# Moving a product, its hash and its place in a step of a fused attention and mixture-of-experts kernel

## Chip, cores and metric

The kernel runs on one core of a Trainium2 chip. The metric is the device time of one execution in microseconds (us); three runs of the kernel before have a median of 731.03 us (730.82 to 731.37).

## Reference

Two batches of 8 heads, 768 positions and 64 dimensions go through attention restricted by a hash: `proj` gives 6 sign bits per query and key, and a pair counts only where all bits agree.

```python
q_bucket = np.sum((np.einsum('bhsd,dk->bhsk', q, proj) > 0) * powers, axis=-1)   # k alike
scores = np.where(mask, scale * q @ k.T, -1e9); attn = softmax(scores); attn @ v
```

The result, 1536 rows of 512, goes through 4 dense experts of 512 x 1024 x 512 with a ReLU, and the outputs are summed with row weights `p = domain_probs / sum`.

## The kernel before

**Tiling.** A head is worked on in 6 tiles of 128 queries; a tile is a *step*, and heads are counted 0 to 15 over both batches (8 to 15 are the second batch). `attention()` (line 589) is a generator: at step i it walks the letters of `ORDER` (line 45), each letter a stage with its own lag (lines 21 to 32) behind the scores, so several heads are in flight.

- S (`stage_s`, 397): scores of a tile on TensorE, 4 matmuls into a `big` PSUM buffer (2 of them); VectorE reads it with the mask's minimum (L409).
- E (420): exponential on ScalarE (L425) with the row sums.
- N (430): reciprocals of a head's row sums (L436, L437), written out as a `row` from the SP queue (L439). R (441): the rows read back, spread over 64 partitions (L450).
- Heads 0 to 8 are *mixed* (`LIGHT_FROM = 9`): T (457) turns a tile of probabilities on TensorE with 6 matmuls against the identity (L470), and ScalarE and VectorE copy it to a `pt` buffer.
- Heads 9 to 15, the *late* ones, turn by another way: X (481) transposes 32 x 32 blocks on VectorE (L490) and after three tiles writes them to a scratch tensor (`scr`, L496); Y (502) reads them back in four DMAs (L507) into a `pt` buffer. There are 3 `pt` buffers; a read-back waits until the product of the head before has freed its buffer.
- V (514): the product of probabilities and values, 24 matmuls in column tiles (L525) into `pv`. For mixed heads it comes in two parts at lags 4 and 6 after the head's last tile, for late heads at once at lag 8. U (534) copies `pv` out (L552, L554); M (556) multiplies with the reciprocals on GpSimd (L565).
- P: one step of `prep_head` (301) for the next head, on the turned inputs `xt`: the high part on ScalarE (L330) with three GpSimd copies, the low part on VectorE (L333), the *hash* (four small matmul passes in column tiles into `hps`, L346), its Sign on ScalarE (L356), and the mask rows on GpSimd (L361, L369). P also issues the loads of q, k (L206, twice removed head) and v (L222).

**Order of work.** Instructions are issued to each engine in the order in which the program is written (`manual_schedule`), so engines and the SP queue, which issues nearly every DMA, are in-order lists. Until the first batch's attention is done the main loop (line 1018) only steps attention; then the experts of batch 0 (`moe`, 774) run with the attention of batch 1 between them. Each `yield` gives a cost; after each block of 12 matmuls (1960 for the first layer, 2600 for the second) the loop at line 1034 steps attention while its summed yields are below the experts' times `n_att / n_moe` = 112404 / 250240. A step's scores yield 1363, a turning by T 654, a head's prep of a late head 978 in all, a step after the last tile 2500.

**Weights.** `split_w` (684) turns a loaded weight tile `ws` (512 KB, two buffers) into a high part (VectorE cast, L699) and a low part (GpSimd, L692); its calls stand between the blocks, and two of seven issue the next load on SP (`load_w`, L681). Load (u, i, c) is chunk c of layer i+1 for unit u.

Of the kernel before, what the change touches and what calls it, by code (L numbers as in the profile page):

```python
# [8 lines left out]
F32 = mybir.dt.float32  # L9
# [10 lines left out]
ATT_PACE = 1.0  # L20
LAG_E = 1
SPLIT_AT = (1, 0)
HASH_AT = (3, 1)
LAG_N = 3
LAG_R = ((6, 4), (7, 6))
LAG_T = 3
LAG_X = 2
LAG_Y = 4
LAG_V = ((4, 6), (8,))
LAST_V = (4, 5)  # L30
LAG_U = (3, 1)
LAG_M = (10, 10)
# [9 lines left out]
W_SPLIT = 40  # L42
W_STEP = 6
PREP_AT = 0
ORDER = "TXSUVMEYNRP"
LIGHT_FROM = 9
DRAIN = 2500
SPLIT_FIRST = 3
# [3 lines left out]
def tile_lsh_attention__then__domain_moe(  # L52
# [52 lines left out]
    def one(name):  # L105
        return ps1.tile([P, 512], F32, tag="one", name=name)
# [15 lines left out]
    def two(t):  # L122
        return t.rearrange("p (a n) -> p a n", a=2)
# [107 lines left out]
    def copy_pool(dst, src):  # L231
        nc.gpsimd.tensor_scalar(out=dst, in0=src, scalar1=1.0, scalar2=1.0, op0=ALU.mult, op1=ALU.mult)
# [63 lines left out]
    def turn_blocks(b, h):  # L296
        tqk = loaded.pop((0, b, h))
        xts[b, h] = ld.tile([P, S], F32, tag="tqk", name="xt")
        nc.vector.transpose(out=xts[b, h], in_=tqk.rearrange("p c r d -> p (c r d)"))

    def prep_head(b, h):
        second = (b, h) == (0, 1)
        q1, al, ah, k2 = stack_tiles(b, h)

        def copies():
            for rows in (slice(0, D), slice(D, P)):
                copy_pool(q1[rows], ah[0:D].bitcast(F32))
            copy_pool(k2[0:D], ah[D:P].bitcast(F32))

        if second:  # L310
            for ps, sl in zip(in_psum, halves):
                split_half(ah[:, sl], al[:, sl], ps[:, :NH])
            copies()
            yield 654
            yield 0
            ps = [one("hps1") for _ in range(2)]
            for j, (w, a) in enumerate(((phi, ah), (plo, ah), (phi, al))):
                for i, sl in enumerate(halves):
                    nc.tensor.matmul(ps[i][:MKE, :NH], w, a[:, sl], start=j == 0, stop=j == 2)
            copy_pool(ah[0:D], al[D:P].bitcast(F32))  # L320
            for i, sl in enumerate(halves):
                nc.scalar.activation(
                    k2[D:MKE, sl], ps[i][D:MKE, :NH], ACTF.Sign, bias=sgn_bias[D:MKE], scale=SGN_SCALE
                )
            yield 978
        else:
            xt = xts.pop((b, h))
            for _ in range(SPLIT_AT[not mixed(b, h)]):
                yield 0
            nc.scalar.activation(two(ah), two(xt), ACTF.Copy, scale=qk_scale)  # L330
            copies()
            yield 0
            nc.vector.scalar_tensor_tensor(  # L333
                out=two(al),
                in0=two(xt),
                scalar=qk_scale,
                in1=two(ah).bitcast(F32),
                op0=ALU.mult,
                op1=ALU.subtract,
            )  # L340
            copy_pool(ah[0:D], al[D:P].bitcast(F32))
            for _ in range(HASH_AT[not mixed(b, h)] - SPLIT_AT[not mixed(b, h)] - 1):
                yield 0
            hps = one("hps")
            for i, sl in enumerate(halves):
                nc.tensor.matmul(  # L346
                    hps[i * D : i * D + MKE - D, :NH],
                    pf[:, : MKE - D],
                    xt[:, sl],
                    start=True,  # L350
                    stop=True,
                    tile_position=(0, i * D),
                )
            for i, sl in enumerate(halves):
                rows = slice(i * D, i * D + MKE - D)
                nc.scalar.activation(  # L356
                    k2[D:MKE, sl], hps[rows, :NH], ACTF.Sign, bias=sgn_bias[rows], scale=SGN_SCALE
                )
            if not mixed(b, h):
                yield 978  # L360
        nc.gpsimd.tensor_scalar(  # L361
            out=al[D:MKE],
            in0=k2[D:MKE].bitcast(F32),
            scalar1=1.0,
            scalar2=bit_mul[D:MKE],
            op0=ALU.add,
            op1=ALU.mult,
        )
        copy_pool(k2[MQ:MQE], al[MK:MKE].bitcast(F32))  # L369
        yield 978 if mixed(b, h) and not second else 0  # L370

    xhi = {}
    xlo = {}
# [17 lines left out]
    def mixed(b, h):  # L391
        return b * H + h < LIGHT_FROM
# [121 lines left out]
    def stage_v(b, h, part, n_parts):  # L514
        if part == 0:
            pvs[b, h] = one("pv")
        ps = pvs[b, h]
        n = NT // n_parts
        for c in range(part * n, (part + 1) * n):
            for g in range(2):  # L520
                rows = slice(g * D, (g + 1) * D)
                dst = ps[rows, :GN]
                if not heavy(b, h, g * G):
                    dst = dst.rearrange("p (a q) -> p a q", q=32)
                nc.tensor.matmul(  # L525
                    dst,
                    vvs[b, h][:, c],
                    pts[b, h, g][c],
                    start=c == 0,
                    stop=c == NT - 1,  # L530
                    tile_position=(0, g * D),
                )
# [47 lines left out]
    def v_lags(b, h):  # L580
        return LAST_V if (b, h) == (0, H - 1) else LAG_V[not mixed(b, h)]

# [6 lines left out]
    def attention():  # L589
        n = len(seq)  # L590
        prep = [iter(())]

        def do(op, i):
            if op == "N":
                j = i - LAG_N
                if 0 <= j < n:
                    stage_n(*seq[j])
            elif op == "R":
                for b in range(B):
                    for odd in range(2):  # L600
                        j = i - LAG_R[b][odd]
                        if 0 <= j < n and (seq[j][0], seq[j][1] % 2) == (b, odd):
                            stage_r(*seq[j])
            elif op == "T":
                j = i - LAG_T
                if 0 <= j < n and heavy(*seq[j]):
                    stage_t(*seq[j])
                    return 654
            elif op == "X":
                j = i - LAG_X  # L610
                if 0 <= j < n and not heavy(*seq[j]):
                    stage_x(*seq[j])
            elif op == "Y":
                j = i - LAG_Y
                if 0 <= j < n and j % G == G - 1 and not heavy(*seq[j]):
                    b, h, t = seq[j]
                    stage_y(b, h, t // G)
            elif op == "S":
                if i < n:
                    b, h, t = seq[i]  # L620
                    if t == 0:
                        x = hseq.index((b, h))
                        prep[0] = prep_head(*hseq[x + 1]) if x + 1 < len(hseq) else iter(())
                    stage_s(b, h, t)
                    return 652 + 4270 // NT
                return DRAIN
            elif op == "V":
                for bh, lag in ended(i):
                    for part, at in enumerate(v_lags(*bh)):
                        if lag == at:  # L630
                            stage_v(*bh, part, len(v_lags(*bh)))
            elif op == "U":
                for bh, lag in ended(i):
                    if lag == u_lag(*bh):
                        stage_u(*bh)
            elif op == "M":
                for (b, h), lag in ended(i):
                    for g in range(NT // G):
                        if h % 2 and lag == (u_lag(b, h) if (b, h) == (0, H - 1) else LAG_M[b] + g):
                            stage_m(b, h, g)  # L640
            elif op == "E":
                j = i - LAG_E
                if 0 <= j < n:
                    stage_e(*seq[j])
            elif op == "P":
                if i < n:
                    b, h, t = seq[i]
                    c = next(prep[0], None) if t >= PREP_AT else None
                    x = hseq.index((b, h))
                    if t == NT - 1 and x + 2 < len(hseq) and in_blocks(*hseq[x + 2]):  # L650
                        turn_blocks(*hseq[x + 2])
                    if t == QK_AT and x + 2 < len(hseq):
                        load_qk(*hseq[x + 2])
                    if t == NT - 1 and x + 1 < len(hseq):
                        load_v(*hseq[x + 1])
                    return c
            return None

        for i in range(n + LAG_M[1] + 3):
            for op in ORDER:  # L660
                c = do(op, i)
                if c is not None:
                    yield c
# [410 lines left out]
```

## Time and profile before

| | |
|---|---|
| median of 3 runs | 731.03 us |
| profiled execution | 729.12 us, span of its instructions 727.4 us |
| mean granted TensorE clock | 0.997 |
| busy: TensorE, VectorE, ScalarE, GpSimd | 711.5, 483.0, 296.6, 303.0 us |
| chain that ended last, by engine | PE 88%, DVE 3%, DMA 3%, ACT 2% |
| DMA | 83.05 MB, 41% of 16 engines on the SP queue |

The first batch's attention takes the first 131 us; batch 0's experts with batch 1's attention reach to about 470 us, and the experts of batch 1 fill the rest. Busy times overlap; matmuls are pipelined with modelled ends, so a busy TensorE is not TensorE at its peak. PE is TensorE, PEld its weight loads, DVE VectorE, ACT ScalarE, POOL GpSimd, and SPq the DMA queue of SyncE. A line number such as L525 is a line of the kernel. In the chain each piece is followed back to what released it.

### The profile page before, as it was taken

The page shows a single profiled execution, that of the slowest core. Times are in us where ns is not written, and L with a number is a line of the kernel's source. Part 1 is how long each engine was busy: PE and PEld are TensorE (multiplying, and loading weights), DVE is VectorE, ACT ScalarE, POOL GpSimd, SP SyncE. Part 2 cuts the span into 40 slices and gives each one's busy share as a digit, 9 for nine tenths or more (in the row PEclk, how much of TensorE's full clock was granted, in tenths as well). Part 3 has the DMA queues.
Part 4 walks back from the last instruction along what each step waited for, and adds up shares of the span by engine and source line. Part 5 has one row for each costly group of instructions (what it writes and reads, how often), then busy time and mean ns, then how long its engine had stood idle before and what let it go on. Part 6 is the DMA issues. An engine that isn't in the chain of part 4 may idle for free.

```text
span 727.4 us, 10195 instructions
## 1 busy us (share of the span) xinstructions
PE 711.5 (98%) x3786; PEld 602.5 (83%) x3786; DVE 483.0 (66%) x800; ACT 296.6 (41%) x588; POOL 303.0 (42%) x283
## 2 busy tenths in 40 slices
PE   8999999999999999999979999999999999999998
PEld 6766766887978878798768889898998989899896
DVE  6898898456857566668524333986768576685863
ACT  6888888432433324323111111543425334352440
POOL 6359577413354253424213243933434243342420
PEclk9999999999999999999999999999999999999999
DMA  5323253227858869786466121142113221112202
GB/s 146 66 46 88 58 117 80 39 77 187 232 138 225 234 175 236 212 267 195 134 199 163 37 71 67 59 146 87 59 59 87 58 87 58 59 59 88 87 1 87
DMA packets 88641, 83.05 MB, mean 114 GB/s; under 512 B 53008, under 2 KB 55568, under 8 KB 88592
## 3 DMA queue, kind: packets, MB, share of 16 engines
q1 hardware_dynamic: 87568, 82.08, 41.0%
q8 instruction: 30, 0.49, 0.3%
q10 hardware_dynamic: 1024, 0.33, 0.2%
q14 instruction: 19, 0.16, 0.1%
HBM read 62.68 MB, written 19.71 MB: 113 GB/s over the span
## 4 chain that ended last, share of the span: by engine, by line
PE 88%; DVE 3%; DMA 3%; ACT 2%; POOL 1%; issue 1%; SPq 1%; DVEq 0%; POOLq 0%; ACTq 0%
PE mps L731 12%; PE mps L732 12%; PE mps L733 12%; PE pv L525 8%; PE mps L791 5%; PE mps L792 5%; PE mps L793 5%; PE ptps L470 4%; PE sps L404 4%; PE sps L402 4%; DMA ws<-in_moe_w_dram 3%; PE mps L946 2%; PE mps L942 2%; PE mps L945 2%; PE pd L942 2%; PE pa L946 2%
## 5 line engine op out<-in xcount | busy, mean ns | idle before, releaser
L731 PE MATMUL mps<-w2hi,hh 128*128 128x512 f32 (+1 forms) x388 | 151.0, 389 | 0.0
L733 PE MATMUL mps<-w2hi,hl 128*128 128x512 f32 (+1 forms) x388 | 150.5, 388 | 0.0
L732 PE MATMUL mps<-w2lo,hh 128*128 128x512 f32 (+1 forms) x388 | 150.4, 388 | 0.0
L725 DVE SCALAR_TENSOR_TENSOR acc<-mps,pe,acc 128x512 f32<-128x512 f32 (+1 forms) x85 | 63.0, 741 | 70.9 <-PE mps L733 70.4
L425 ACT ACTIVATE p<-p,nb 128x768 f32<-128x768 f32 x96 | 89.5, 933 | 35.6 <-DVE p L409 35.1
L797 ACT ACTIVATE hh<-mps 128x384 fp32r<-128x384 f32 x64 | 31.4, 491 | 169.8 <-PE mps L793 169.8
L409 DVE TENSOR_SCALAR_CACHE_REDUCE p<-sps 128x768 f32<-128x768 f32 x96 | 90.3, 942 | 15.1 <-PE sps L404 13.5
L791 PE MATMUL mps<-xs,w1hi 128*128 128x384 f32 x256 | 87.6, 342 | 4.7 <-DVE hl L798 4.7
L792 PE MATMUL mps<-xs,w1hi 128*128 128x384 f32 x256 | 86.6, 338 | 0.6 <-POOL xs L570 0.6
L793 PE MATMUL mps<-xs,w1lo 128*128 128x384 f32 x256 | 86.6, 338 | 0.0
L733 PEld LDWEIGHTS mps<-w2hi,hl 128*128 128x128 f32 x388 | 72.9, 188 | 15.7
L928 POOL TENSOR_TENSOR w2lo<-ws,w2hi 128x512 fp32r<-128x512 f32 x32 | 40.6, 1289 | 108.3 <-ACT w2hi L927 108.3
L731 PEld LDWEIGHTS mps<-w2hi,hh 128*128 128x128 f32 x388 | 72.9, 188 | 15.0 <-issue 1.2
L732 PEld LDWEIGHTS mps<-w2lo,hh 128*128 128x128 f32 x388 | 72.9, 188 | 13.9
L692 POOL TENSOR_TENSOR w1lo<-ws,w1hi 128x512 fp32r<-128x512 f32 x32 | 41.2, 1290 | 84.9 <-DVE w1hi L699 76.8
L692 POOL TENSOR_TENSOR w2lo<-ws,w2hi 128x512 fp32r<-128x512 f32 x32 | 41.2, 1288 | 82.5 <-DVE w2hi L699 66.3
L798 DVE SCALAR_TENSOR_TENSOR hl<-mps,hh 128x384 fp32r<-128x384 f32 x64 | 35.4, 555 | 59.1 <-ACT hh L797 58.8
L525 PE MATMUL pv<-pt,tv 128*64 128x384 f32 x288 | 67.3, 492 | 0.0
L402 PE MATMUL sps<-ah,q 128*128 128x384 f32 x192 | 54.0, 362 | 1.8 <-DVE p L409 1.8
L791 PEld LDWEIGHTS mps<-xs,w1hi 128*128 128x128 f32 x256 | 48.6, 190 | 8.2 <-DVE hl L798 5.0
L887 POOL TENSOR_TENSOR w1lo<-ws,w1hi 128x512 fp32r<-128x512 f32 x24 | 37.1, 1547 | 36.5 <-ACT w1hi L883 22.5
L470 PEld LDWEIGHTS ptps<-ident,p 128*128 128x128 f32 x324 | 36.4, 140 | 18.3 <-ACT p L425 8.2
(137 smaller groups left out, 1392.2 us busy)
## 6 DMA issues: line engine op xcount, KB each, us to landing
ws<-in_moe_w_dram SPq DMA_DIRECT2D x64, 512.0 KB, 4.0
scr<-t SPq DMA_DIRECT2D x14, 1152.0 KB, 8.6
pt<-scr SPq DMA_DIRECT2D x56, 288.0 KB, 6.1
tv<-in_v_dram SPq DMA_DIRECT2D x16, 192.0 KB, 3.7
tqk<-in_q_dram SPq DMA_DIRECT2D x30, 96.0 KB, 3.0
out_dram<-acc SPq DMA_DIRECT2D x11, 256.0 KB, 2.0
tqk<-in_k_dram SPq DMA_DIRECT2D x28, 96.0 KB, 3.1
rdb<-row SPq DMA_DIRECT2D x14, 192.0 KB, 6.2
```

Of the source, the lines that this page charges most:

```text
L402: nc.tensor.matmul(ps[:, i, :NH], q1[:, sl], k1[:, i * NH : (i + 1) * NH], start=True, stop=False)
L409: nc.vector.tensor_scalar(out=two(pt), in0=ps[:, :, :NH], scalar1=MASKED, scalar2=MASKED, op0=ALU.min, op1=ALU.min, accum_out=nb,)
L425: nc.scalar.activation(pt, pt, ACTF.Exp, bias=nb, scale=-1.0, accum_out=dens[b, h, r][:, o : o + 1])
L470: nc.tensor.transpose(ps[:, c * P : (c + 1) * P], pt[:, (a + c) * P : (a + c + 1) * P], ident)
L525: nc.tensor.matmul(dst, vvs[b, h][:, c], pts[b, h, g][c], start=c == 0, stop=c == NT - 1, tile_position=(0, g * D),)
L692: nc.gpsimd.tensor_tensor(out=lo[:, c - 1], in0=st[c - 1], in1=hi[:, c - 1].bitcast(F32), op=ALU.subtract)
L731: nc.tensor.matmul(ps, hh[:, ts], w2hi[:, f, cs], start=n == 0, stop=False)
L732: nc.tensor.matmul(ps, hh[:, ts], w2lo[:, f, cs], start=False, stop=False)
L733: nc.tensor.matmul(ps, hl[:, ts], w2hi[:, f, cs], start=False, stop=n == FC - 1)
L791: nc.tensor.matmul(ps[:, :SB], w1hi[:, kk, fs], xhi[b, kk][:, sl], start=kk == 0, stop=False)
L792: nc.tensor.matmul(ps[:, :SB], w1hi[:, kk, fs], xlo[b, kk][:, sl], start=False, stop=False)
L793: nc.tensor.matmul(ps[:, :SB], w1lo[:, kk, fs], xhi[b, kk][:, sl], start=False, stop=kk == KD - 1)
```

## The change

- `LAG_V` of late heads goes from 8 to 7 and V moves ahead of S in `ORDER`. `u_lag` follows the product, so U of late heads goes from 9 to 8; M, N, R, X, Y and the loads keep their lags.
- The hash of late heads moves from the second step of their prep to the first, beside the high part; the Sign follows it at once.
- For mixed heads the hash's matmuls are put on a list (`due`) at the end of the step in which the low part is made, and are issued in the next step's V, that is after T and the product and ahead of S; the Sign stays where it was.
- The yields of a prep change: late heads 654 + 978 in place of 978 in all, mixed heads 654 + 978 + 978 in place of 978. The number of yields is the same.

```diff
-HASH_AT = (3, 1)
+HASH_AT = (2, 0)
-LAG_V = ((4, 6), (8,))
+LAG_V = ((4, 6), (7,))
-ORDER = "TXSUVMEYNRP"
+ORDER = "TXVSUMEYNRP"
+    due = []
+    hashed = {}
+
+    def hash_of(b, h, xt):
+        hps = one("hps")
+        for i, sl in enumerate(halves):
+            nc.tensor.matmul(
+                hps[i * D : i * D + MKE - D, :NH],
...
+        hashed[b, h] = hps
+
+    def sign_of(b, h):
+        hps = hashed.pop((b, h))
+        for i, sl in enumerate(halves):
+            rows = slice(i * D, i * D + MKE - D)
+            nc.scalar.activation(
+                heads[b, h][3][D:MKE, sl], hps[rows, :NH], ACTF.Sign, bias=sgn_bias[rows], scale=SGN_SCALE
+            )
...
             xt = xts.pop((b, h))
...
+            late = b * H + h > H
+            steps = {}
+            steps.setdefault(SPLIT_AT[late], []).append("hi")
+            steps.setdefault(SPLIT_AT[late] + 1, []).append("lo")
+            steps.setdefault(HASH_AT[late], []).append("hash")
+            for at in range(max(steps) + 1):
+                if at:
+                    yield 654 if at == 1 else 0
+                for what in steps.get(at, ()):
...
+                    elif late:
+                        hash_of(b, h, xt)
+                        sign_of(b, h)
+                    else:
+                        due.append((b, h, xt))
+            yield 978
+            if not late:
+                sign_of(b, h)
...
-        yield 978 if mixed(b, h) and not second else 0
+        yield 0 if second or b * H + h > H else 978
...
                         if lag == at:
                             stage_v(*bh, part, len(v_lags(*bh)))
+                while due:
+                    hash_of(*due.pop())
```

## Rows read from the trace of the kernel before

**Rows 1.** Waits of TensorE in 130:430 (us in total, times, longest us)

```profile
PE mps L791 <- DVE hl L798: 4.7, 1, 4.7
PE sps L402 <- DVE p L409: 1.5, 2, 1.2
```

**Rows 2.** Windows (length, busy by engine (count), granted clock, DMA share, GB/s)

```profile
80.00:100.00 20.00, 18.98 (x124) 12.79 (x120) 18.17 (x34) 16.36 (x37) 17.85 (x19) 1.00 0.26 57
...
280.00:300.00 20.00, 18.51 (x102) 16.19 (x102) 18.60 (x33) 8.47 (x17) 10.35 (x9) 1.00 0.82 223
...
360.00:380.00 20.00, 15.33 (x83) 12.12 (x83) 3.66 (x6) 2.34 (x5) 1.46 (x2) 0.97 0.61 181
380.00:400.00 20.00, 20.00 (x96) 18.01 (x95) 9.54 (x18) 1.97 (x4) 7.55 (x6) 0.95 0.62 148
```

**Rows 3.** Chain that ended last, 355:385 (start us, us, what)

```profile
361.35 4.07 PE pv L525 x24
...
368.39 9.13 DMA ws<-in_moe_w_dram
...
377.62 0.14 DVE w2hi L699
...
378.56 0.66 PE mps L791
```

**Rows 4.** Timeline of the SP queue, 130:420 (start us, us)

```profile
164.69 0.38 SPq L681 DMA_DIRECT2D ws<-in_moe_w_dram  x1
165.18 1.83 SPq L507 DMA_DIRECT2D pt<-scr  x4
...
219.71 0.59 SPq L439 DMA_DIRECT2D row<-rd  x1
220.41 0.38 SPq L681 DMA_DIRECT2D ws<-in_moe_w_dram  x1
220.89 1.95 SPq L507 DMA_DIRECT2D pt<-scr  x4
...
237.59 1.75 SPq L507 DMA_DIRECT2D pt<-scr  x4
...
271.16 0.51 SPq L681 DMA_DIRECT2D ws<-in_moe_w_dram  x1
...
365.39 1.73 SPq L507 DMA_DIRECT2D pt<-scr  x4
```

**Rows 5.** Chain in 255:300, pieces of the repeating blocks

```profile
257.92 0.35 PE sps L402 x2
...
258.87 0.23 PE mps L732
...
291.31 0.17 PE mps L792
```

**Rows 6.** Chain in 200:215, a hash right behind a product

```profile
209.06 0.65 PE hps L346 x4
```

**Rows 7.** Timeline of VectorE round the reciprocal of head 10

```profile
216.13 0.75 DVE L725 SCALAR_TENSOR_TENSOR acc<-mps,pe,acc 128x512 f32<-128x512 f32 x1 [1.64 <-PE mps L733]
...
218.04 0.19 DVE L437 RECIPROCAL rd<-den 128x6 f32<-128x6 f32 x1
```

**Rows 8.** L507 to landing, of four reads: windows 163:168, 220:223, 236:240

```profile
DMA to landing us min/median/max: 4.4/5.7/7.1
...
DMA to landing us min/median/max: 6.2/7.3/8.5
...
DMA to landing us min/median/max: 3.4/5.0/6.3
```

**Rows 9.** Timeline of TensorE round a hash that stands alone (start us, us)

```profile
141.87 0.34 PE L793 MATMUL mps<-xs,w1lo 128*128 128x384 f32 x1
...
142.92 0.44 PE L791 MATMUL mps<-xs,w1hi 128*128 128x384 f32 x1
143.20 0.34 PE L792 MATMUL mps<-xs,w1hi 128*128 128x384 f32 x1
```

More of the change, by code (lines that the diff above doesn't have):

```diff
@@ L299, in turn_blocks @@
         nc.vector.transpose(out=xts[b, h], in_=tqk.rearrange("p c r d -> p (c r d)"))
+    due = []
[5 more added lines that the diff above has]
+                hps[i * D : i * D + MKE - D, :NH],
+                pf[:, : MKE - D],
+                xt[:, sl],
+                start=True,
+                stop=True,
+                tile_position=(0, i * D),
+            )
[6 more added lines that the diff above has]
+                heads[b, h][3][D:MKE, sl], hps[rows, :NH], ACTF.Sign, bias=sgn_bias[rows], scale=SGN_SCALE
+            )
     def prep_head(b, h):
@@ L327, in prep_head @@
             xt = xts.pop((b, h))
[L328 to L360, printed above, removed]
+            late = b * H + h > H
+            steps = {}
+            steps.setdefault(SPLIT_AT[late], []).append("hi")
+            steps.setdefault(SPLIT_AT[late] + 1, []).append("lo")
@@ new lines, in prep_head @@
+            steps.setdefault(HASH_AT[late], []).append("hash")
[3 more added lines that the diff above has]
+                for what in steps.get(at, ()):
+                    if what == "hi":
+                        nc.scalar.activation(two(ah), two(xt), ACTF.Copy, scale=qk_scale)
+                        copies()
+                    elif what == "lo":
+                        nc.vector.scalar_tensor_tensor(
+                            out=two(al),
+                            in0=two(xt),
+                            scalar=qk_scale,
+                            in1=two(ah).bitcast(F32),
+                            op0=ALU.mult,
+                            op1=ALU.subtract,
+                        )
+                        copy_pool(ah[0:D], al[D:P].bitcast(F32))
+                    elif late:
[3 more added lines that the diff above has]
+                        due.append((b, h, xt))
```

## The prediction, made before the kernel after was run

> **What bounds the kernel now.** I read the share of each engine first, then the windows, the waits of TensorE, the chain through its longest wait, and last the DMA issues of the SP queue. TensorE (PE) works almost without a break: between 130 and 430 us it waits for long only once, 4.7 us for `hl` [rows 1]. The windows place the idle time [rows 2]: 1.49 us in 280:300, 4.67 us in 360:380, and in the first batch 1.02 us in 80:100. So this change can gain only what such holes hold, and lose whatever new holes it opens.
>
> The chain shows how the 4.7 us came about [rows 3]. The product of head 14 (L525) runs 361.35 to 365.4; SP's L507, which reads probabilities back into a `pt` buffer that this product must free, follows at 365.39; behind it in SP's order stand a write to scratch and the weight load L681 at 368.39, which takes 9.13 us to land. VectorE, in order, sits in the cast L699 of those weights, `hl` behind it comes late, and PE resumes at 378.56. The hole of 280:300 is the same figure one cycle earlier: `ws` issued at 271.16 behind L507 [rows 4]. After the long hole the granted clock is 0.97 and 0.95 of full over two windows [rows 2], that is PE at 1.2 instead of 2.4 GHz for about 3.2 us, or 0.08 x 20 = 1.6 us lost.
>
> **How the order moves.** Positions below are us of PE work since the mixture experts began, worked out from the yields: an expert block of 12 matmuls is 12 x 0.17 or 12 x 0.23, a score tile twice 0.35 [rows 5], a product 4.07 [rows 3], a hash 0.65 [rows 6]; attention is stepped while its own counts are under 0.449 of the experts' (1,960 or 2,600 a block). So a late step with its scores, 1,363 counts, comes once per 3,035 expert counts, some 1.3 blocks or 3.3 us, and with its share of products, hashes and prep about every 5 us. The walk of the kernel before puts head 14's product at 226.3; plus 135 it is the 361.35 of the chain. Two things act on it. LAG_V 8 to 7, with V ahead of S, brings a product a step and a score tile forward. But a late head now yields 654 + 978 where it yielded 978, so a head costs 9,810 counts instead of 9,156 and the experts run 7% further per head. Together the products of heads 9 to 15 move from 73.3, 101.6, 132.5, 163.6, 194.6, 226.3, 265.5 to 66.4, 98.1, 131.1, 162.2, 195.3, 223.5, 263.4: little against the experts, and head 13's is even later. What changes is the order on SP.
>
> **The two weight waits (gain).** Before, the first read-back of head 12 and its scratch write stand ahead of weight load (3,1,0), and that read-back needs head 11's product, still a step away. After, the load comes at 131.1, ahead of the read-back at 138.6. Behind a scratch write issued near 127 it lands by 137, taking the 10.0 us of the load at 271.16 [rows 4]; its cast stands at 141.4. Head 15's read-back and load (5,1,0) swap alike: issue near 219.5, landing by 229.5, cast at 232.4. Both waits go, with 4.4 and 2.9 us to spare: -1.5 - 4.7 - 1.6 = -7.8 us.
>
> **The read-backs of the same head (loss).** A head's second read-back is ready only when its reciprocals are written (L439, ahead of it on SP), and now has one step less before its product. Before, the end of a block to the end of the reciprocal took about 2.1 us on VectorE (acc at 216.13, L437 until 218.23 [rows 7]); the row went out at 219.71 because SP was held by `tqk` loads, and the four reads at 220.89 [rows 4]. The last of four reads is issued about 1.3 us after the first. Landing, counted from the first issue, took 1.3 + 6.3 = 7.6 us (the four at 237.59), and with a weight load just ahead 1.3 + 7.1 = 8.4 (at 165.18) to 1.4 + 8.5 = 9.9 (at 220.89) [rows 4, 8]. By the walk, with 2 to 3 us for VectorE and 0.4 per issue, the four reads of heads 9 to 14 begin 7.0, 9.1, 7.7, 8.4, 10.2 and 9.3 us before PE reaches the product. Heads 9 and 12 have a weight load directly ahead of them: waits of 1.4 to 2.9 and 0 to 1.5. Head 10 has one further ahead (I take 0.2), head 13 has one but also the room, heads 11 and 14 have none. I take 2.0 + 0.2 + 0 + 0.8 + 0 + 0 = +3.0 us; the bounds are 0.6 (7.6 for all) and 8.0 (9.9 for all). Behind a waiting product on PE stand S and every later block; VectorE, ScalarE and the experts' evictions wait with it.
>
> A wait of 2 us before a product is between the 1.0 us holes that left the clock at 1.00 [rows 2] and the 4.7 us one that did not; I take no drop. The Trainium skill (TensorE: Matmul & The Clock Gate, Part 1) has it that the throttled state is the default and that activity releases it; a drop behind head 9's wait would by that cost about the 1.6 us again and make the forecast 729.2.
>
> **The late hash (loss).** Four hashes (heads 12 to 15) stood directly behind a product; now S and an expert block lie between. Behind a product a hash takes 0.65 [rows 6]; alone, from the matmul before it (141.87) to the one behind (142.92) pass 1.05 us, less 0.17 is 0.88, and the next spacing is 0.28 instead of 0.17 [rows 9]: 0.34 more, four times, +1.4 us (bounds 0 and 2.0). Its Sign on ScalarE comes a step sooner and POOL's `al` at the same step; neither ends a wait there. U comes a step sooner, M, rows and loads of q and k keep their steps.
>
> **The first batch.** Hash and product stay neighbours and stay at their steps; S comes after them instead of before. The same tiling switches, the same VectorE work and the same buffers lie between two transposes, so I cost it at nothing. The Sign no longer waits for PE, but `al` is queued on POOL behind other work. Bounds -1.5 and +1.5, about the hole of 80:100 and half again. Attention's last drain step ends at 306.8 instead of 297.8 of 330.9; the forced drain stands at 308.8, so the operands of the second layer's fast form are not later: nothing.
>
> Sum: -7.8 + 3.0 + 1.4 = -3.4 us. On the profiled execution, 729.12 (span 727.4 and 1.7 around it), that is 725.7; the median shown, 731.03, is 0.26% above it, and gives **727.6**.
>
> **Rivals.** *A, slower:* the read-backs land late for most heads. Place: PE in front of L525; price: 9.9 us for all gives 8.0 of waits (732.6); if each also starts 1.5 us late, as the row at 219.71 did after 218.23, 16.7 (741.3); middle 735. It decides once the six waits pass 6.4 us. For it speaks that `pt` reads behind other traffic took 9.9; against it, that SP was held then by loads stuck behind a scratch write that itself had waited for the product, which the change removes. *B, same:* one weight wait half survives, since load (5,1,0) still follows a scratch write and its 2.9 us to spare hang on a landing I took from another place: -7.8 + 3.2 + 4.4 = -0.2, 730.8. *C, faster:* every read-back lands in 7.6 us: -7.8 + 1.4 + 0.6 = -5.8, 725.2. The Trainium skill (DMA: Bandwidth & Descriptors, Anatomy of one DMA) gives a transfer about 2.0 us plus its bytes at 436 GB/s, for POOL's path; by it an estimate for the 1.18 MB of four reads is 4.7 us and no product waits. The landings here took 7.6 us and more. *D, not what it says:* the dearer yields eat the step and the order on SP stays, so only the hash is paid: 732.4. Against it stands the walk.
>
> **How the numbers follow.** Forecast 0.42 (own range 725 to 730), A 0.20, B 0.13, C 0.20, D 0.05. About 0.2% (1.5 us) is what a measurement can tell here. Faster by more: 0.38 of the forecast, 0.19 of C and 0.03 of B, 0.60; slower: 0.17 of A, 0.03 of D and 0.02 of B, 0.22; the rest, 0.18, is no difference. The range goes from C with the first batch's 1.5 us gained (723.5) to the middle of A (734.5).
>
> **What would show it.** Right: PE idle of 280:300 and 360:380 gone, clock 1.00 there; `ws` (5,1,0) issued before the L507 that follows head 14's product; PE waits on L525 for `pt` of some 2 us at head 9 and under 1.5 at head 12; hashes alone in the second batch. Wrong: waits of 2 us or more at most products (A), a cast L699 that still waits over 4 us with `hl` behind it (B), or idle in the first 130 us changed by over 1.5 us.

## The result, and the profile after

The kernel after takes **740.13 us** (738.52 to 740.64, 4 runs), the kernel before beside it 730.92 (730.46 to 731.37, 4 runs): a ratio of 1.0122, with an interval of 1.0105 to 1.014. It is slower by 9.2 us, where 727.6 had been forecast and 734.5 was the end of the range. The profiled span is 738.4 us, 11.0 longer than before.

The gain that was forecast is there, and two losses are greater than it. First the waits of TensorE in 130:430 (us in total, times, longest us), which answer to [rows 1]:

```profile
PE pv L546 <- DMA pt<-scr: 7.5, 3, 4.6
```

The wait for `hl` is gone. In its place the product waits for its read-back, at three heads. The windows of the kernel after (length, busy by engine (count), granted clock, DMA share, GB/s), against [rows 2]:

```profile
80.00:100.00 20.00, 18.80 (x117) 12.28 (x117) 17.28 (x34) 17.04 (x35) 16.30 (x18) 1.00 0.31 55
200.00:220.00 20.00, 15.44 (x66) 9.99 (x65) 6.99 (x14) 4.55 (x9) 0.00 (x0) 0.83 0.82 225
280.00:300.00 20.00, 20.00 (x110) 16.93 (x107) 9.90 (x18) 5.08 (x11) 7.03 (x7) 1.00 0.90 230
300.00:320.00 20.00, 17.88 (x93) 14.07 (x92) 12.45 (x23) 7.27 (x15) 6.88 (x7) 1.00 0.69 189
360.00:380.00 20.00, 20.00 (x98) 14.92 (x96) 14.54 (x28) 5.59 (x12) 7.50 (x6) 1.00 0.76 231
380.00:400.00 20.00, 20.00 (x112) 19.36 (x111) 7.80 (x16) 4.90 (x11) 5.17 (x4) 1.00 0.64 182
```

280:300, 360:380 and 380:400 are full, at a clock of 1.00: the 7.8 us of the old weight waits came back as worked out. New holes stand in 200:220 (4.56 us, and a granted clock of 0.83, that is some of the window at 1.2 instead of 2.4 GHz) and in 300:320 (2.12). In 80:100 the count tells more than the busy time: 117 matmuls where there were 124.

The timeline of TensorE shows the product of heads 9 and 12 begin, stop after two matmuls, and go on when the read-back has landed:

```profile
203.56 0.86 PE L546 MATMUL pv<-pt,tv 128*64 128x384 f32 x2
208.99 6.23 PE L546 MATMUL pv<-pt,tv 128*64 128x384 f32 x21 [4.56 <-DMA pt<-scr]
...
310.67 0.86 PE L546 MATMUL pv<-pt,tv 128*64 128x384 f32 x2
313.66 4.06 PE L546 MATMUL pv<-pt,tv 128*64 128x384 f32 x22 [2.12 <-DMA pt<-scr]
```

Two matmuls take 0.34 us, so head 9 stood for 208.99 - 203.56 - 0.34 = 5.1 us and head 12 for 2.65; head 11 stood for 1.3 (277.33 to 279.01). That is 9.1 us. Behind the longest one 21 matmuls took 6.23 us; head 12's 22 took 4.06, so 2.4 us went with the clock.

The first batch is the other loss. The same matmul of the experts, the one that waits 0.6 us for `xs` from GpSimd, starts at 133.19 before:

```profile
133.19 0.45 PE L792 MATMUL mps<-xs,w1hi 128*128 128x384 f32 x1 [0.61 <-POOL xs L570]
```

and at 138.65 after:

```profile
138.65 0.44 PE L815 MATMUL mps<-xs,w1hi 128*128 128x384 f32 x1 [0.60 <-POOL xs L591]
```

**The sum:** +5.5 first batch, +9.1 waits for read-backs, +2.4 clock, +1.4 for four hashes that now stand alone (below, with e9), -7.8 weight waits make +10.6 of the 11.0 us. The other 0.4 I cannot place.

### The profile page after: what moved, and what is told of

It is laid out like the page before. It is cut to its first block, busy times and chain, and to the rows that moved or that the text cites. A ratio compares the mean times of both kernels' runs of the same rounds, so it can differ in the third digit from the quotient of the medians.

```text
span 738.4 us, 10204 instructions
## 1 busy us (share of the span) xinstructions
PE 718.2 (97%) x3786; PEld 604.5 (82%) x3786; DVE 478.1 (65%) x800; ACT 298.3 (40%) x588; POOL 300.6 (41%) x283
## 4 chain that ended last, share of the span: by engine, by line
PE 86%; DMA 4%; DVE 3%; ACT 3%; POOL 2%; issue 1%; SPq 0%; DVEq 0%; POOLq 0%; ACTq 0%
PE mps L754 11%; PE mps L756 11%; PE mps L755 11%; PE pv L546 8%; PE mps L814 5%; PE mps L815 5%; PE mps L816 5%; DMA pt<-scr 4%; PE sps L423 4%; PE sps L425 3%; PE ptps L491 3%; PE mps L969 2%; PE mps L965 2%; PE mps L968 2%; PE pd L965 2%; PE pa L969 2%
## 5 line engine op out<-in xcount | busy, mean ns | idle before, releaser
L546 PE MATMUL pv<-pt,tv 128*64 128x384 f32 x288 | 72.6, 512 | 8.6 <-DMA pt<-scr 7.5
L546 PEld LDWEIGHTS pv<-pt,tv 128*64 128x64 f32 x288 | 27.1, 142 | 42.3 <-issue 34.5
L425 PE MATMUL sps<-k,al 76*128 76x384 f32 x192 | 49.9, 340 | 1.0 <-POOL k L232 0.6
```

The lines of the kernel that those rows point to most:

```text
L425: nc.tensor.matmul(ps[:, i, :NH], q2[0:MQE, sl], k2[0:MQE, i * NH : (i + 1) * NH], start=False, stop=True)
L546: nc.tensor.matmul(dst, vvs[b, h][:, c], pts[b, h, g][c], start=c == 0, stop=c == NT - 1, tile_position=(0, g * D),)
```

## Experiments

The first expert matmul (130.58 in the trace before, 136.04 after) is a second reading of each run: how long the first batch took. In parentheses stand the ratio to the kernel before that ran beside it, and the interval of that ratio; the kernel before took 729.5 to 730.9 us there, so medians of different rows compare only to about 1 us.

**Undoing the order of a step, in one batch and in both.** The first 54 steps are those of heads 0 to 8.

```diff
 e1, from the kernel after
-            for op in ORDER:
+            for op in "TXSUVMEYNRP" if i < 54 else ORDER:
 e2, from the kernel after
-ORDER = "TXVSUMEYNRP"
+ORDER = "TXSUVMEYNRP"
```

> The changed kernel with the old order in the steps of heads 0 to 8 alone (V and the hash behind S again), the second batch as changed. Theory: V ahead of S costs the first batch some 5.5 us, because VectorE and then ScalarE, which is nearly as full as TensorE there, get their next scores later; so 740.1 - 5.5 = 734.6 us, the experts start near 133 us again, and the product of head 9 still waits about 5 us for its read-back. Rival: the first batch lost its time to something else in the prep (the Sign, the yields, the held hash buffer): 739 to 740 us and a start of the experts near 138 us.

> The changed kernel with V behind S in every step (the old order of stages), late products still at lag 7. Theory: the first batch gets its 5.5 us back, and the late products stand a score tile and an expert block later, 13 us instead of 7 behind the first read-back issue of head 9 and 14.6 instead of 8.4 at head 12, longer than the 11.8 and 11.0 us that those took to land; so their waits of 9.1 us and the 2.5 us of slow clock go too, while the weight loads stay ahead of the read-backs: 740.1 - 5.5 - 11.6 = 723 us. Rival: the weight waits of 280:300 and 360:380 hang on the product's place and come back: 731 us.

e1 took 734.96 us (1.0075, 1.0058 to 1.0092; expert start 131.15); e2 took **722.12** (0.9895, 0.988 to 0.9909). Both were as expected. The order of the first batch costs 5.2 us by the medians and 4.9 by the expert start, and with the old order in both batches the rest of the change (lag 7, yields, hash) gains 7.5 us. The waits on `pt` are gone in e2, and the reason is plain when head 9's second read-back and product are put side by side: first issue at 192.07 and product at 198.64 in e1, 6.6 us; 191.64 and 204.41 in e2, 12.8 us. One letter in `ORDER` is worth more than the 0.7 us of the score tile it passes, because the loop runs expert blocks between a step's scores and what follows.

**The product's place in the first batch alone, from the kernel before.**

```diff
 e3
-            for op in ORDER:
+            for op in "TXVSUMEYNRP" if i < 54 else ORDER:
 e7
+            for op in "XVTSUMEYNRP" if i < 54 else ORDER:
```

> The kernel before with V ahead of S in the steps of heads 0 to 8 alone; hash, yields and second batch as before. Theory: the place of V alone costs the first batch: 731 + 5.5 = 736.4 us, experts start near 138 us. Rival: the hash ahead of S is what cost it: 731 us.

> The kernel before with V ahead of T as well as of S in the steps of heads 0 to 8 (order V, T, S in place of T, S, V), rest as before. Scores, products and turnings then follow each other as in the kernel before (S V T S), only the product's index is one step earlier. Theory: what costs the first batch is that T stands directly behind S and ahead of the product (S T V S): it asks for exponentials and copies 2 us sooner and leaves VectorE and ScalarE without new scores during the product. Then this order costs little, 731 to 733 us. Rival: the product itself is too soon behind the copies of its last turned tile: 736 us or more.

e3: 737.24 (1.0103, 1.0088 to 1.0118; start 138.13), as expected. e7: 740.34 (1.0139, 1.0122 to 1.0156; start 140.50), a miss: I had expected the product to cost little if it stood ahead of the turning too; the rival, 736 or more, came. So the loss belongs to the product's place, without any move of the hash or change of a yield. In e7 the product waits 3.8 us for ScalarE's `pth`, seven times.

How a head loses time is seen in the timelines of TensorE round the first part of a product. Before:

```profile
65.94 0.54 PE L525 MATMUL pv<-pt,tv 128*64 128x384 f32 x1
...
77.92 0.96 PE L470 MATMUL ptps<-ident,p 128*128 128x128 f32 x6
78.64 0.60 PE L402 MATMUL sps<-ah,q 128*128 128x384 f32 x2
79.07 0.51 PE L404 MATMUL sps<-k,al 76*128 76x384 f32 x2
79.51 0.54 PE L525 MATMUL pv<-pt,tv 128*64 128x384 f32 x1
```

and in e3:

```profile
68.12 0.54 PE L525 MATMUL pv<-pt,tv 128*64 128x384 f32 x1
...
80.56 0.61 PE L402 MATMUL sps<-ah,q 128*128 128x384 f32 x2
81.01 0.51 PE L404 MATMUL sps<-k,al 76*128 76x384 f32 x2
81.68 0.87 PE L470 MATMUL ptps<-ident,p 128*128 128x128 f32 x6 [0.16 <-ACT p L425]
82.88 0.54 PE L525 MATMUL pv<-pt,tv 128*64 128x384 f32 x1 [0.33 <-ACT pth L476]
```

A head takes 82.88 - 68.12 = 14.76 us instead of 13.57. From a turning to the next operation pass 1.20 instead of 0.72 us, since the product asks for ScalarE's copy of its head's last tile (turned a step earlier), and the turning itself starts 0.67 behind a pair of score matmuls (81.01 to 81.68) instead of 0.36 (77.56 to 77.92 before), since ScalarE's exponential is late. VectorE and ScalarE in e3 in that stretch:

```profile
77.33 0.96 DVE L409 TENSOR_SCALAR_CACHE_REDUCE p<-sps 128x768 f32<-128x768 f32 x1 [2.38 <-PE sps L404]
```

```profile
80.60 0.94 ACT L425 ACTIVATE p<-p,nb 128x768 f32<-128x768 f32 x1 [0.43 <-DVE p L409]
...
81.53 0.92 ACT L330 ACTIVATE ah<-xt,qk_scale 128x768 fp32r<-128x768 f32 x1
82.36 0.47 ACT L476 ACTIVATE pth<-ptps 128x384 f32<-128x384 f32 x1
```

Turning and product run one behind the other while VectorE has no score tile to read (2.38 us), then VectorE and ScalarE have to catch up, and the copy `pth` stands behind an exponential and the high part `ah`. Over 20:130 VectorE waits for scores 8.2 us in the kernel before and 19.4 in the kernel after:

```profile
DVE p L409 <- PE sps L404: 8.2, 12, 1.8
```

```profile
DVE p L430 <- PE sps L425: 19.4, 16, 2.2
```

**Is it the copies, or the alternation?** Five kernels try to take away what the product waits for, by older copies (e10, and e11 as its control in the old order), by a later first part (e12), or by clearing ScalarE's queue (e13, e14; the low part moves along with the high part).

```diff
 e10 from e3, e11 from e6 (below)
-LAG_V = ((4, 6), (8,))
+LAG_V = ((5, 7), (8,))    e10
+LAG_V = ((5, 7), (7,))    e11
 e12 from e3
+LAG_V = ((5, 6), (8,))
 e13 and e14 from e3
-SPLIT_AT = (1, 0)
+SPLIT_AT = (0, 0)    e13
+SPLIT_AT = (2, 0)    e14
```

> The kernel before with the product ahead of the scores in the first batch (e3, 737.2) and the mixed heads' products at lags 5 and 7 in place of 4 and 6, so that the tiles that a product reads were turned a step earlier and their copies are done. If the loss of e3 is that the product asks for copies too fresh, it goes: 729.5 to 732. If the loss is that VectorE and ScalarE get no scores while turning and product run on TensorE one behind the other, it stays: 735.5 to 738.

> The fastest kernel so far (e6: before with the late heads' product at lag 7 alone, 722.0) with the mixed heads' products at lags 5 and 7. If copies too fresh cost time in the first batch already in the old order, 1 to 2 us less, 720 to 721. If in the old order the scores between turning and product cover the copies, no change, 721.5 to 722.5, or up to 1 us more where the last head of the first batch comes out later.

> e3 (before with the product ahead of the scores in the first batch, 737.2) with the mixed heads' product at lags 5 and 6 in place of 4 and 6, so that its first part no longer asks for the copy that ScalarE makes late. No pt buffer is held longer than in e3, so e10's new wait stays away. If ScalarE's late copy is the main part of the loss (0.5 us a head), 733 to 735, with the waits of PE on ACT pth gone. If the loss is in how the engines alternate and the wait only shows where it comes out, 736 to 738.5, with another wait in its place.

> e3 with the mixed heads' high part ah (0.92 us of ScalarE) one step earlier, so that it no longer stands between an exponential and the copy of the last turned tile that the product waits for. If that queue is the main part, 733 to 735.5 and a shorter wait of PE on ACT pth. If not, 736 to 738.5.

> e3 with the high part one step later, behind that copy, with the hash in the step of the low part. If ScalarE's queue ahead of the copy is the main part, 733 to 735.5; a new wait for the next head's operands (ah, al through GpSimd), which now come a step later, could take some of it back. If not, 736 to 738.5.

| kernel | us | ratio (interval) | expert start | TensorE's main wait in 20:130 |
|---|---|---|---|---|
| e3 | 737.24 | 1.0103 (1.0088 to 1.0118) | 138.13 | `pth` from ScalarE 1.0 |
| e10 | 739.99 | 1.0136 (1.0121 to 1.0151) | 140.31 | `ptps` for VectorE's `pt` 6.0 |
| e12 | 746.48 | 1.023 (1.0214 to 1.0245) | 148.32 | `pt` from VectorE 9.3 |
| e13 | 741.21 | 1.0157 (1.014 to 1.0175) | 142.49 | `pth` from VectorE 4.4 |
| e14 | 736.79 | 1.0098 (1.0083 to 1.0113) | 138.04 | `k` from GpSimd 3.0 |

None got the time back. e10, e12 and e13 came out above the ranges of both of their readings, and so did e11; only e14 fell into one, that of "if not". e10 confounded itself. Turnings, products and hashes write to the same four buffers in PSUM (`one`, line 105), and with the later lags U, which frees the product's buffer, comes behind the next head's hash instead of ahead of it. In e10 U's two copies run at 69.80 and 72.46, and the hash holds its buffer until the Sign has read it, from 71.23 on; the second half of a turning in between waits for VectorE's copy of the turning before, which stands behind the low part (L333, 1.54 us):

```profile
69.33 0.85 PE L346 MATMUL hps<-xt,pf 128*44 128x384 f32 x4
...
71.61 0.55 PE L470 MATMUL ptps<-ident,p 128*128 128x128 f32 x3 [0.95 <-DVE pt L474]
```

e11 shows that the lags cost by themselves, since they took 730.38 in the *old* order (0.9999, 0.999 to 1.0009; start 139.24) where e6 takes 722.01 (start 130.44), with the same wait, 6.3 us in six times. That the shared buffers are the reason is read from the kernel and one place of the trace; no run takes them away. In e12 U keeps its step, and it is the worst: the two parts now follow in neighbouring steps, and the product waits for VectorE. e14 did what it was made for: the wait on ScalarE's `pth` is gone from the list, and a longer one on GpSimd came in its place, 3.0 us. The waits in 20:130 of e14:

```profile
DVE p L409 <- PE sps L404: 24.5, 20, 2.4
...
PE sps L404 <- POOL k L232: 3.0, 3, 1.3
```

and of e12:

```profile
DVE p L409 <- PE sps L404: 27.8, 13, 3.9
...
PE pv L525 <- DVE pt L474: 9.3, 7, 1.6
```

What TensorE waits for changes from kernel to kernel. What does not change is VectorE's idle time for scores, 19 to 28 us in all six kernels with the product between turning and scores (the kernel after, e3, e10, e12, e13, e14) against 8.2; in e7 it is 6.8, but there VectorE waits 14.3 us for turned tiles. That fits the alternation of the engines, and no single copy that could be taken out of the product's way gave the time back. It is not proof: each of these edits brought a wait of its own, and e11 loses time in the old order with 12.1 us of that idle time. Which of VectorE, ScalarE and the buffers would have to be relieved, and by how much, these runs do not settle.

**What removes the weight waits: the lag or the yields?**

```diff
 e4, from the kernel after
-LAG_V = ((4, 6), (7,))
+LAG_V = ((4, 6), (8,))
 e5, from the kernel before (first yield behind the high part)
-            yield 0
+            yield 0 if mixed(b, h) else 654
 e6, from the kernel before
-LAG_V = ((4, 6), (8,))
+LAG_V = ((4, 6), (7,))
```

> The changed kernel with the late products back at lag 8, still ahead of S. Theory: the read-backs have landed before the product, so its waits and the slow clock go (11.6 us) and the first batch's 5.5 us stay; the two weight loads stay ahead of the first read-backs on SP by the dearer yields alone, so their waits stay away: 728.5 us. Rival: with lag 8 the read-back waits on SP for the product again and the weights behind it are late: about 735 to 737 us, with a wait of L814 for hl.

> The kernel before with one edit: a late head's prep yields 654 + 978 instead of 0 + 978, as in the changed kernel; lag, order and hash as before. Theory: the yields alone put the weight loads (3,1,0) and (5,1,0) ahead of the first read-backs on SP, so both weight waits go, and the product at lag 8 has 20 us after the reciprocals and never waits: 731 - 8.4 = 722.6 us. Rival: it is the product's earlier place that frees the read-back and with it the weights: then nothing changes, 731 us.

> The kernel before with LAG_V of late heads 7 instead of 8 and nothing else. Theory: with the old yields the first read-backs of heads 12 and 15 still stand ahead of the weight loads on SP, so the two waits stay in some part, though the read-back now waits less for its product; the hashes lose their place behind the products (+1.4): 727 to 732 us. Rival: the lag alone takes the weight waits away: 723 us.

e4: 728.72 (0.9985, 0.9976 to 0.9994). e5: 724.8 (0.9926, 0.9911 to 0.9941). e6: **722.01** (0.9887, 0.9872 to 0.9902), a miss of the theory and a hit of its rival. e4 came as expected. e5 gained 5.8 us, 2.2 short of its theory: the 4.7 us wait is gone and 360:380 is full, but 260:300 has 3.0 us of idle time, which its waits list as 1.3 for the Sign (as in e2, see e9 below), 0.9 for VectorE's reading of scores and 0.8 for `hl`. So dearer yields alone remove the long weight wait, and the shorter lag alone removes both (280:300 and 360:380 are full in e6), in two ways: the yields turn the order on SP round, as the prediction had it; the lag leaves the order and moves all of it forward. SP in e6:

```profile
265.96 1.74 SPq L507 DMA_DIRECT2D pt<-scr  x4
267.79 0.38 SPq L496 DMA_DIRECT2D scr<-t  x1
268.21 0.51 SPq L681 DMA_DIRECT2D ws<-in_moe_w_dram  x1
```

The weight load still stands behind read-back and scratch write, but at 268.21 instead of 271.16 [rows 4], and the load (5,1,0) at 362.17 instead of 368.39 [rows 3]; neither makes TensorE wait any more. With V behind S the read-back has time: head 9's four reads are issued at 186.52 and its product starts at 198.63, 12.1 us later, and no wait on `pt` is listed. e4 shows the same from the other side: reads at 196.98, as in the kernel after, and the product at 210.44 without a wait.

**The price of a hash by itself,** from e2:

```diff
-HASH_AT = (2, 0)
+HASH_AT = (2, 1)
```

> The kernel of e2 (everything of the change but the order of a step) with the late heads' hash one step later, so that four of them stand by themselves again instead of next to a product. If a hash by itself costs what the prediction charged (4 x 0.34 us), 723.5 (723.2 to 724.1). If that price does not exist, because e6 with hashes by themselves was as fast as e2, 722.1 (721.6 to 722.6). A gain would speak for a Sign that came too soon in e2.

722.0 (0.9886, 0.9871 to 0.99) against 722.12: no difference. But this is not yet "no price", since e2 has a wait that e9 has not. In e2, behind the hash of head 13, TensorE's next matmul waits until ScalarE's Sign has read the hash:

```profile
238.93 0.81 PE L307 MATMUL hps<-xt,pf 128*44 128x384 f32 x4
241.06 0.44 PE L814 MATMUL mps<-xs,w1hi 128*128 128x384 f32 x1 [1.32 <-ACT k L321]
```

That is 2.13 us from one to the other, where 0.74 pass behind the next head's hash (272.23 to 272.97): 1.39 us lost. The same hash in e9, alone (it starts at 244.19, between the first two lines):

```profile
243.92 0.34 PE L816 MATMUL mps<-xs,w1lo 128*128 128x384 f32 x1
...
244.97 0.44 PE L814 MATMUL mps<-xs,w1hi 128*128 128x384 f32 x1
245.24 0.34 PE L815 MATMUL mps<-xs,w1hi 128*128 128x384 f32 x1
```

1.05 us and then 0.27, where matmuls of this block follow each other at 0.17: the hash adds 0.98 us, against the 0.65 of a hash behind a product [rows 6], so 0.33 to 0.34 more, four times 1.4 us. The Sign that came too soon in e2 hides the price, as the last sentence of the expectation allowed for. From the first expert matmul to the end e2 takes 589.55 us and e9 589.75. e6, with its hashes alone and no such wait, agrees (589.73). The kernel after has the four hashes alone, with the same spacings (1.05 to 1.10 us), and no wait for the Sign: it pays the 1.4 us. No run shows the price in its time alone.

**Why the read-back lands late.** In the kernel after a weight load stands directly ahead of the second read-backs of heads 9, 12 and 13, which take 11.8, 10.9 and 10.7 us from first issue to last landing; those of heads 10, 11, 14 and 15, without one, take 8.4 to 8.9. e8 (from e1) counts the weight loads that fall due in a slot and issues them behind that slot's attention (the lines that reset the count are left out here).

```diff
+    held = [None]
...
+        if held[0] is None:
+            load_now()
+        else:
+            held[0] += 1
...
+                for _ in range(held[0] or 0):
+                    load_now()
```

> The kernel of the first run (735.0 us: old order in the first batch, second batch as changed) with each weight load issued after attention's DMAs of the same slot instead of ahead of them, so that the read-backs of heads 9 and 12 have no weight load in front of them. Theory: a weight load directly ahead costs a read-back about 2 us of its landing; the product of head 9 waits 2 us instead of 4 and more, that of head 12 almost nothing, and the slow clock behind head 9 stays away or gets shorter: 729 to 731 us. Rival: the landing is long because of the scratch write and the loads behind it that share the engines, whatever the order: 735 us, waits on pt as they were.

740.85 (1.0147, 1.0128 to 1.0166), a miss of both readings. The chain of e1 at head 9:

```profile
193.47 9.77 DMA pt<-scr
...
203.48 2.55 PE pv L546 x8
```

and of e8:

```profile
191.01 1.19 DVE w2hi L730
...
193.26 0.34 SPq L460
...
195.08 7.52 DMA pt<-scr
...
202.70 2.79 PE pv L546 x7
```

From its issue the last read takes 7.52 us without the weight load ahead and 9.77 with it: that half of the theory held, 2.3 us. But the weights, now late, hold VectorE in `w2hi` ahead of the reciprocal, the row goes out at 193.26 instead of 191.14, and the product gains only 0.8 us. Other heads got worse (head 12 stands idle for 5.94 us, since its reads begin 4.7 us ahead of the product instead of 8.0 and the load of the slot before is still ahead of them), to 10.0 us of waits for `pt` in all against 5.8 in e1.

## Why the prediction was wrong

**The weight waits: right.** -7.8 us had been summed and the windows show all of it. `ws` of (5,1,0) is issued ahead of the read-back that follows head 14's product, as the walk had it:

```profile
371.86 3.70 SPq L704 DMA_DIRECT2D ws<-in_moe_w_dram  x2
380.16 1.75 SPq L528 DMA_DIRECT2D pt<-scr  x4
```

The swap was not needed for it, though (e6), and yields that swap the order leave smaller waits if the lag stays at 8 (e5).

**The read-backs: mechanism and place right, term mis-sized, +3.0 against +9.1 and 2.4.** The starts were right within 0.4 us for five of the six heads: from first issue to product 7.0, 9.1, 7.7, 8.4, 10.2 and 9.3 us were worked out, and 6.6, 9.1, 7.4, 8.0, 10.5 and 10.6 measured (head 9: 196.97 to 203.56). The step that failed is the landing, "with a weight load just ahead 1.3 + 7.1 = 8.4 [...] to 1.4 + 8.5 = 9.9". Head 9's SP queue and chain in the kernel after:

```profile
196.04 0.34 SPq L460 DMA_DIRECT2D row<-rd  x1
196.49 0.38 SPq L704 DMA_DIRECT2D ws<-in_moe_w_dram  x1
196.97 2.32 SPq L528 DMA_DIRECT2D pt<-scr  x4
```

```profile
198.37 10.37 DMA pt<-scr
...
208.99 4.07 PE pv L546 x11
```

198.37 + 10.37 - 196.97 = 11.8 us from the first issue to the last landing. Head 12 took 10.9 by the same count and head 11, which I had thought free of a wait, some 9. The bound had been the slowest of three read-backs of the kernel before [rows 4, 8], and 9.9 was not even the slowest of that trace. Two others there, one with two weight loads and a row ahead of it and one with a weight load directly ahead, took 1.5 + 8.8 = 10.3 and 1.8 + 8.8 = 10.6 us:

```profile
250.57 2.00 SPq L507 DMA_DIRECT2D pt<-scr  x4
...
DMA to landing us min/median/max: 6.3/7.7/8.8
```

```profile
382.29 2.41 SPq L507 DMA_DIRECT2D pt<-scr  x4
...
DMA to landing us min/median/max: 6.9/8.1/8.8
```

With 10.6 us the waits of heads 9 and 12 would have come out at 3.6 and 2.2 instead of 2.0 and 0.8; the 11.8 of head 9 was beyond any read-back of the trace before. The 4.7 us that the figure of the Trainium skill (DMA: Bandwidth & Descriptors, Anatomy of one DMA) had given as an estimate was reached by none of these read-backs. Rival A, "the read-backs land late for most heads", named this mechanism with a point of 6.4 us from which it decides; the waits passed it, at three heads of the six.

**The clock: "I take no drop".** It was taken for a wait of 2 us at head 9. Head 9 waited 5.1, more than the 4.7 us wait of the kernel before [rows 1], and 2.4 us went at the lower level; behind the 2.65 us of head 12 the granted clock stayed at 1.00 (300:320). The rule of the Trainium skill that was weighed against it (TensorE: Matmul & The Clock Gate, Part 1: throttled by default, released by activity) would have charged 1.6, and the trace agrees with its direction: 1.00 ahead of the wait, 0.83 in the window behind it.

**The late hash: +1.4 was taken, and the spacings bear it out.** Each of the four hashes of the kernel after stands alone, with the spacings of [rows 9]. The equal times of e2 and e9 don't speak against it, since a wait of e2 makes up for it.

**The first batch: "I cost it at nothing" is the second step that failed, 5.5 us** beside the 6.1 of the read-backs (8.5 with the clock). The sign named for it came: TensorE's idle time in the first 130 us went from 5.5 to 8.5 us. The argument counted what lies between two turnings and found it the same. It named no cover for the new place of the product. That the place costs the time is shown (e1, e3); how is argued. Before, the scores (0.7 us) stood between the last turning and the product, time in which ScalarE finished the copies, and VectorE got its next tile ahead of the product and not behind it. VectorE was busy 18.17 and ScalarE 16.36 of 20 us there [rows 2], so neither had much room to make up a pause, and these rows were there to see it. The bound of 1.5 us was put at one and a half old holes, which no mechanism set.

Rival A's direction and place were right, its price was short of the first batch; with that, A's middle of 735 would have come to 740.5. That this is so near the measured 740.13 is in part luck, since A had its waits at most heads and no clock.

## What to carry to other kernels

When a stage is moved ahead of the one that feeds the other engines, look at how full those engines are in that stage. Here, with VectorE busy 18.2 and ScalarE 16.4 of 20 us, a reordering that left TensorE's count the same cost 5 to 17 us, and which wait showed changed with each edit. A product that must find a transfer landed needs a margin taken from all landings of the trace, those with another load directly ahead above all; three of them gave no bound. Two kernels of equal time need not show that a term is nothing: look whether one of them has a wait that the other has not. A change of several parts is worth splitting: the lag alone (one number) gives 722.01, 1.1% faster than the kernel before and 18 us better than the whole change.

## What was unexpected

- The four reads of a head's second read-back (1.18 MB) took 8.4 to 11.8 us from the first issue to the last landing in the kernel after; the four heads with no weight load directly ahead were the fastest. In e1 and e8 the load directly ahead is worth 2.3 us of the last read's landing.
- Here waits could be exchanged for one another: e14 took away every listed wait of the product on ScalarE's copies and gained 0.45 us of the 7.6 that e3 loses.
- Lags 5 and 7 cost 8.4 us in the old order (e11 against e6), all of it ahead of the first expert matmul.
- In e2 the Sign of one hash costs TensorE 1.39 us, as much as four hashes that stand alone.
